# The last block of a weight load in six partition pieces: the tail of a gated attention and FFN kernel on Trainium2

## The chip, the cores and the metric

The kernel runs on one core of a Trainium2 chip. The metric is the device time of one execution in microseconds (us). It is taken from several runs, and their median counts. One further execution is recorded by the hardware profiler, and all rows below come from that one.

## What is computed

The reference mixes two branches over a batch of two tokens (D = 448) with a sigmoid gate: attention over a cache of 4096 positions with 16 heads of 256, and a feed-forward layer with 1792 hidden units. Everything is in float32.

```python
x = A_x
g = _sigmoid((x * gate_w).sum(-1, keepdims=True))
# a: q = x @ wq; scores = q . k_cache * 256 ** -0.5; softmax; o = p . v_cache; a = o @ wo
a = _A_ref(x, A_k_cache, A_v_cache, A_wq, A_wo)
# b: h = x @ w1 + b1; h = relu(h) ** 2; b = h @ w2 + b2
b = _B_ref(x, B_w1, B_b1, B_w2, B_b2)
return g * a + (1 - g) * b
```

The K and V caches are 268 MB of the 290 MB that are read, so nearly all of the run is one long stream of loads.

## The kernel before

The work is cut into 16 rounds; a round is two heads of one batch entry. Each round loads a K tile and a V tile of 128 partitions x 16384 floats. VectorE multiplies K by q in place (`times_q`, L282) and sums the rows (`row_sums`, L288); a maximum over partitions and an exponential give the softmax; TensorE multiplies the probabilities with V (`values`, L333). Three large tiles (`kp0`, `kp1` for K in turn, `vp` for V) fill the memory on the chip, so that each load waits until the tile that it overwrites has been used.

All large loads are issued by hand, in program order, on the queue of SP (SyncE). Each load is tied to one of eight landing semaphores (`DMAHW0` to `DMAHW7`), in turn, and these are shared by all loads and stores. A load is issued only when the load that had the same semaphore before it, eight places earlier, has landed.

The end of the program is what matters here. When the last K tile has been used, the remaining weights go into its place, `kp1`: `load_wo` (L115) brings the last part of wo, then `load_v` (L132) the last V tile into `vp` in five loads cut at `V_CUTS = (32, 48, 56, 60)` of 64 rows, and `load_w2` (L98) all of w2. w2 is laid out as 128 partitions x 14 blocks x 448 floats (`"(p c) n -> p c n"`): partition p holds 14 consecutive rows of w2, and block c is one of them from each partition, 1792 bytes per partition. `W2_CUTS = (2, 6, 10, 13)` makes five loads of it: blocks 0-1, 2-5, 6-9, 10-12 and the single block 13 (224 KB).

TensorE's order at the end is written by hand too: the five pieces of the last `values`, then `late_w2(0, 2)`, the turn of the last attention output (`take_turn`), `late_wo` for two heads, and `late_w2(2, FC)` for blocks 2 to 13. `late` (L379) multiplies a 128x2 operand with four slices of 112 columns of a block and adds into the accumulator `fin`. Each block is four such matrix products, which the trace shows as eight weight loads and eight matmuls. ScalarE copies `fin` out (L498), and SP and ScalarE store one batch row each (L500, L501).

Of the kernel before, what the change touches and what calls it, by code (L numbers as in the profile page):

```python
# [16 lines left out]
def kernel(  # L17
# [14 lines left out]
    nc = tc.nc  # L32
# [13 lines left out]
    FC = F // P  # L46
# [6 lines left out]
    W2_CUTS = (2, 6, 10, 13)  # L53
# [33 lines left out]
    w2_v = w2.rearrange("(p c) n -> p c n", c=FC)  # L87
    w2_sb = {}

    def load_w2():  # L90

        at = HJ * D
        tv = kp[last % 2][:, at:at + FC * D].rearrange("p (c n) -> p c n", n=D)
        for c in range(FC):
            w2_sb[c] = tv[:, c, :]
        cuts = [0, *W2_CUTS, FC]
        for lo, hi in zip(cuts, cuts[1:]):
            nc.sync.dma_start(tv[:, lo:hi, :], w2_v[:, lo:hi, :])  # L98

# [375 lines left out]
    load_wo(NG - 1, last)  # L477
    vt_next = load_v(i + 1, vp, V_CUTS)
    load_w2()
    values(i, vt, 0, NK // 4)  # L480
    mt = maximum(i + 1)
# [8 lines left out]
    cuts = [0, *(c // 2 for c in V_CUTS), NK // 2]  # L490
# [38 lines left out]
```

## Time and profile before

| what | value |
|---|---|
| median of 3 runs | 680.91 us (680.66 to 680.99) |
| the profiled execution's own time | 680.71 us |
| its span on the core | 678.9 us |
| read from memory | 289.56 MB, 427 GB/s over the span |
| VectorE busy | 573.2 us (84%) |
| TensorE matmul busy | 245.9 us (36%) |
| ScalarE busy | 35.5 us (5%) |

The span runs from the first to the last event on the core; the execution's own time is 1.8 us longer. The chain of waits is read back from the last instruction, at each step to whatever released it. The DMA share is the mean over the 16 engines that move data: 0.25 means that about four of the sixteen are at work. PE is TensorE's matmul, PEld its weight loads, DVE VectorE, ACT ScalarE, SP SyncE, and a q behind a name (SPq) is that engine's instruction queue. PE's busy times are modelled and overlap.

### The profile page before, as it was taken

What the parts mean: (1) busy time and instruction counts of PE and PEld (TensorE: products, weight loads), DVE (VectorE), ACT (ScalarE), POOL (GpSimd) and SP (SyncE); (2) the same over time, 40 slices, a digit from 0 to 9 for tenths busy, and PEclk for the clock granted to TensorE, in tenths of its full rate; (3) what the DMA queues carried; (4) which work ended last, traced back from release to release, by engine and by line L of the source; (5) the groups of instructions that cost most, each with busy time, mean ns of one, the idle gap of its engine ahead of it and who ended that gap; (6) DMA issues with size and microseconds to landing.
All of it is one profiled execution on the core that took longest, in us unless ns stands there. A gap on an engine that the chain in (4) does not pass through costs nothing.

```text
span 678.9 us, 3814 instructions
## 1 busy us (share of the span) xinstructions
PE 245.9 (36%) x1658; PEld 78.9 (12%) x1658; DVE 573.2 (84%) x150; ACT 35.5 (5%) x116; POOL 0.7 (0%) x6
## 2 busy tenths in 40 slices
PE   2522250503308541240515644050512550602476
PEld 1100210100104110010101301010100310100122
DVE  3069999999899995979989895998989799999920
ACT  0001000000001000000000100000000200100000
POOL 0000000000000000000000000000000000000000
PEclk9956575665757656575856578575655775755789
DMA  9999999999999999999999999999999999999996
GB/s 379 440 421 441 440 430 444 432 440 437 429 436 407 452 432 432 432 433 432 432 430 432 436 432 433 432 437 432 432 432 432 412 458 413 426 456 432 399 423 267
DMA packets 7628, 289.80 MB, mean 427 GB/s; under 512 B 950, under 2 KB 1084, under 8 KB 2364
## 3 DMA queue, kind: packets, MB, share of 16 engines
q1 hardware_dynamic: 7448, 289.54, 98.9%
q8 instruction: 13, 0.21, 0.1%
q10 hardware_dynamic: 164, 0.02, 0.0%
q14 instruction: 3, 0.02, 0.0%
HBM read 289.56 MB, written 0.00 MB: 427 GB/s over the span
## 4 chain that ended last, share of the span: by engine, by line
DVE 47%; DMA 44%; issue 6%; PE 3%; ACT 0%; SPq 0%; DVEq 0%; ACTq 0%
DMA kp<-in_A_k_cache_dram 32%; DVE kp L282 25%; DVE s L288 21%; DMA vp<-in_A_v_cache_dram 9%; DMA kp<-in_B_w_dram 2%; PE po_buf L333 2%; PE mt L296 0%; DVE pw L434 0%; PE fin L379 0%; ACT pw L307 0%; DVE m L292 0%; PE sum L313 0%; DVE nb L302 0%; SPq L77 0%; DVE hb L270 0%
## 5 line engine op out<-in xcount | busy, mean ns | idle before, releaser
L282 DVE TENSOR_TENSOR kp<-kp,q 128x8192 f32<-128x8192 f32 (+2 forms) x34 | 278.2, 8182 | 53.2 <-DMA kp<-in_A_k_cache_dram 53.2
L288 DVE TENSOR_REDUCE s<-kp 128x32 f32<-128x8192 f32 x32 | 277.9, 8686 | 1.1
L333 PE MATMUL po_buf<-vp,pw 128*16 128x512 f32 (+1 forms) x960 | 140.9, 747 | 219.1 <-DMA vp<-in_A_v_cache_dram 219.1
L333 PEld LDWEIGHTS po_buf<-vp,pw 128*16 128x16 f32 (+1 forms) x960 | 31.0, 112 | 324.2 <-issue 248.3
L296 PE MATMUL mt<-ident,m 128*64 128x64 f32 x64 | 7.3, 317 | 138.9 <-DVE m L292 138.9
L374 PE MATMUL acc<-kp,oT 128*2 128x448 f32 x48 | 26.8, 730 | 18.8 <-issue 18.8
L307 ACT ACTIVATE pw<-s,nb 64x64 f32<-64x64 f32 x32 | 11.1, 347 | 388.6 <-DVE nb L302 388.4
L296 PEld LDWEIGHTS mt<-ident,m 128*64 128x64 f32 x64 | 4.8, 192 | 149.6 <-issue 127.6
L355 PE MATMUL ot<-rl,shared 128*128 128x8 f32 x96 | 17.0, 307 | 3.8 <-ACT shared L350 3.4
L355 PEld LDWEIGHTS ot<-rl,shared 128*128 128x128 f32 x96 | 16.1, 253 | 7.2 <-ACT shared L350 7.2
L238 PE MATMUL pq<-qs,ident 128*64 128x256 f32 x64 | 14.1, 529 | 0.7 <-ACT qs L226 0.7
L200 PE MATMUL ph<-vp,xT 128*4 128x448 f32 x28 | 7.2, 679 | 17.3 <-DMA vp<-in_B_w_dram 17.3
L333 PE MATMUL po_buf<-kp,pw 128*8 128x512 f32 x64 | 9.6, 752 | 8.7 <-DMA kp<-in_A_v_cache_dram 8.7
L302 DVE TENSOR_REDUCE nb<-mt 128x1 f32<-128x64 f32 x16 | 3.6, 224 | 10.7 <-PE mt L296 10.7
L350 ACT ACTIVATE shared<-po_buf 128x512 f32<-128x512 f32 x12 | 6.5, 594 | 86.5 <-PE po_buf L333 81.1
L200 PE MATMUL po_buf<-vp,xT 128*4 128x512 f32 x56 | 7.8, 714 | 4.9 <-DMA vp<-in_A_wq_dram 4.9
L241 ACT ACTIVATE q<-pq 128x256 f32<-128x256 f32 x16 | 6.1, 383 | 62.5 <-PE pq L238 62.3
L374 PEld LDWEIGHTS acc<-kp,oT 128*2 128x2 f32 x48 | 4.8, 103 | 38.9 <-issue 38.9
L319 DVE RECIPROCAL rc<-sum 128x8 f32<-128x8 f32 (+1 forms) x5 | 1.0, 196 | 9.2 <-PE sum L313 9.2
L307 ACT ACTIVATION_READ_ACCUMULATOR pw<-s,nb 64x1 f32 x32 | 5.9, 184 | 0.0
L434 DVE MEMSET pw<- 128x512 f32 x10 | 4.8, 485 | 0.6
L238 PEld LDWEIGHTS pq<-qs,ident 128*64 128x64 f32 x64 | 4.4, 176 | 4.2 <-issue 2.3
(61 smaller groups left out, 58.1 us busy)
## 6 DMA issues: line engine op xcount, KB each, us to landing
kp<-in_A_k_cache_dram SPq DMA_DIRECT2D x4, 4096.0 KB, 27.6
vp<-in_A_wq_dram SPq DMA_DIRECT2D x1, 7168.0 KB, 19.5
kp<-in_A_wo_dram SPq DMA_DIRECT2D x4, 1792.0 KB, 25.5
vp<-in_A_v_cache_dram SPq DMA_DIRECT2D x1, 4096.0 KB
vp<-in_B_w_dram SPq DMA_DIRECT2D x1, 3136.0 KB
vp<-in_A_v_cache_dram SPq DMA_DIRECT2D x1, 2048.0 KB, 30.7
kp<-in_B_w_dram SPq DMA_DIRECT2D x2, 896.0 KB, 27.4
vp<-in_A_v_cache_dram SPq DMA_DIRECT2D x1, 1024.0 KB
```

Of the source, the lines that this page charges most:

```text
L200: nc.tensor.matmul(out[32 * g:32 * g + 2 * B, :width], xT[:, half, c].rearrange("p s b -> p (s b)"), t[:, (a * n + g) * width:(a * n + g + ...
L238: nc.tensor.matmul(pq[k * PH:(k + 1) * PH, :DH], ident[:, r:r + 1].to_broadcast([P, PH]), qs[:, k * DH:(k + 1) * DH], start=True, stop=True)
L241: nc.scalar.activation(q_sb[i], pq[:, :DH], AF.Copy)
L282: nc.vector.tensor_tensor(kt, kt, q_sb[i].unsqueeze(1).to_broadcast([P, hi - lo, DH]), op=ALU.mult)
L288: nc.vector.tensor_reduce(s_t[i][:, at], rows(kp[i % 2])[:, at, :], axis=AX.X, op=ALU.add)
L296: nc.tensor.matmul(mt[at, :PH], m.to_broadcast([P, PH]), ident[:, at], start=True, stop=True)
L307: nc.scalar.activation(pw[b][at, :, 2 * c:2 * c + 2], s_t[i][at].rearrange("p (m s) -> p m s", s=2), AF.Exp, bias=nb[at], accum_out=rs_t[u ...
L333: nc.tensor.matmul(po[r:r + 4 * n, :], pw[b][:, m, :4 * n], vt[:, 2 * m:2 * m + 2, :].rearrange("p j d -> p (j d)"), start=(k == 0 and b = ...
L350: nc.scalar.activation(o_w[:, s], pv[:, s, lo:lo + nj // 2].unsqueeze(2).to_broadcast([P, nj // 2, HG, HP]), AF.Copy)
L355: nc.tensor.matmul(ptv[:, lo + j, :], ov[:, s, j, :], rl_t[u][:, :, s], start=(s == 0), stop=(s == 1))
L374: nc.tensor.matmul(acc[:, :D], oT[g][:, j, :], wo_sb[g][:, j, :], start=False, stop=(g == NG - 2 and j == HJ - 1))
L434: nc.vector.memset(pw[b], 0.0)
```

## The change

The first four loads of w2 stay. Block 13, which was one load over all 128 partitions, becomes six loads of 64, 36, 14, 8, 4 and 2 partitions, one behind the other on the same queue. Their bytes add up to the same 224 KB and go to the same places.

```diff
-        cuts = [0, *W2_CUTS, FC]
+        cuts = [0, *W2_CUTS]
         for lo, hi in zip(cuts, cuts[1:]):
             nc.sync.dma_start(tv[:, lo:hi, :], w2_v[:, lo:hi, :])
+
+        p = 0
+        for n in (64, 36, 14, 8, 4, 2):
+            nc.sync.dma_start(tv[p:p + n, hi:, :], w2_v[p:p + n, hi:, :])
+            p += n
```

The end of SP's queue before: the load of wo, the five of V, the five of w2, the store. `kp_69` and `kp_70` are the two K tiles, and a name such as `DMAHW4_49` is a landing semaphore that is waited for.

```order
L115 DMA kp_70<-in_A_wo_dram 128x4x896 [waits DMAHW6_49,DVE_49]
L132 DMA vp<-in_A_v_cache_dram 128x8192 [waits DMAHW0_49,PE_49]
L132 DMA vp<-in_A_v_cache_dram 128x4096 [waits PE_49]
L132 DMA vp<-in_A_v_cache_dram 128x2048 [waits DMAHW5_49,PE_49]
L132 DMA vp<-in_A_v_cache_dram 128x1024 [waits PE_49]
L132 DMA vp<-in_A_v_cache_dram 128x1024 [waits DMAHW7_49,PE_49]
L98 DMA kp_70<-in_B_w_dram 128x896
L98 DMA kp_70<-in_B_w_dram 128x1792 [waits DMAHW1_49]
L98 DMA kp_70<-in_B_w_dram 128x1792 [waits DMAHW2_49]
L98 DMA kp_70<-in_B_w_dram 128x1344 [waits DMAHW3_49,DVE_49]
L98 DMA kp_70<-in_B_w_dram 128x448 [waits DMAHW4_49]
L500 DMA out_dram<-shared 4x112 [waits DMAHW6_49,Activation_49]
```

The same place with the change, from the fourth load of w2 on:

```order
L98 DMA kp_70<-in_B_w_dram 128x1344 [waits DMAHW3_49,DVE_49]
L102 DMA kp_70<-in_B_w_dram 64x448 [waits DMAHW4_49]
L102 DMA kp_70<-in_B_w_dram 36x448 [waits DMAHW5_49]
L102 DMA kp_70<-in_B_w_dram 14x448 [waits DMAHW6_49]
L102 DMA kp_70<-in_B_w_dram 8x448 [waits DMAHW7_49]
L102 DMA kp_70<-in_B_w_dram 4x448 [waits DMAHW0_49]
L102 DMA kp_70<-in_B_w_dram 2x448 [waits DMAHW1_49]
L505 DMA out_dram<-shared 4x112 [waits DMAHW3_49,Activation_49]
```

Six issues stand where one stood, and each waits for a landing of its own. The one of 64 partitions waits, as the whole block did, for the second load of the last V tile; those of 36, 14 and 8 wait for the third, fourth and fifth V load, that of 4 for w2's blocks 0-1, that of 2 for w2's blocks 2-5. The store's wait moves from the fourth V load to w2's blocks 10-12.

TensorE's last products (`late_w2`, L379 before and L384 after) before:

```order
L379 MATMUL fin<-kp_70,hT 2x112 [waits DMAHW2_49]
L379 MATMUL fin<-kp_70,hT 2x112 x15
L379 MATMUL fin<-kp_70,hT 2x112 [waits DMAHW3_49]
L379 MATMUL fin<-kp_70,hT 2x112 x11
L379 MATMUL fin<-kp_70,hT 2x112 [waits DMAHW4_49]
L379 MATMUL fin<-kp_70,hT 2x112 x3
L524 UNCONDITIONAL_BRANCH
```

With the change:

```order
L384 MATMUL fin<-kp_70,hT 2x112 [waits DMAHW2_49]
L384 MATMUL fin<-kp_70,hT 2x112 x15
L384 MATMUL fin<-kp_70,hT 2x112 [waits DMAHW3_49]
L384 MATMUL fin<-kp_70,hT 2x112 x11
L384 MATMUL fin<-kp_70,hT 2x112 [waits DMAHW5_49,DMAHW6_49,DMAHW4_49,DMAHW7_49,DMAHW1_49,DMAHW0_49]
L384 MATMUL fin<-kp_70,hT 2x112 x3
L529 UNCONDITIONAL_BRANCH
```

The products and their order are the same. The first product of block 13 waits for six landings instead of one; one wait rides on the instruction, and the other five are carried by three separate wait instructions ahead of it on TensorE's queue.

## Rows read from the trace of the kernel before

**Rows 1.** The page: the span in 40 slices, the DMA lines.

```profile
DMA  9999999999999999999999999999999999999996
GB/s 379 440 421 441 440 430 444 432 440 437 429 436 407 452 432 432 432 433 432 432 430 432 436 432 433 432 437 432 432 432 432 412 458 413 426 456 432 399 423 267
DMA packets 7628, 289.80 MB, mean 427 GB/s; under 512 B 950, under 2 KB 1084, under 8 KB 2364
```

**Rows 2.** The chain of waits, its last steps: start us, us, what.

```profile
587.62 36.40 DMA vp<-in_A_v_cache_dram
...
630.87 26.74 DMA vp<-in_A_v_cache_dram
...
657.67 16.94 DMA kp<-in_B_w_dram
674.60 0.04 issue
674.65 0.99 PE fin L379 x32
...
675.72 0.26 ACT shared L498
```

**Rows 3.** Timeline of TensorE's last stretch: start, length, engine, line, count, idle before.

```profile
665.02 1.05 PE L333 MATMUL po_buf<-vp,pw 128*8 128x512 f32 x8 [0.34 <-DMA vp<-in_A_v_cache_dram]
666.30 1.03 PE L333 MATMUL po_buf<-vp,pw 128*8 128x512 f32 x4 [0.23 <-DMA vp<-in_A_v_cache_dram]
667.58 1.03 PE L333 MATMUL po_buf<-vp,pw 128*8 128x512 f32 x4 [0.25 <-DMA vp<-in_A_v_cache_dram]
668.65 0.30 PEld L379 LDWEIGHTS fin<-kp,hT 128*2 128x2 f32 x16 [0.97 <-DMA kp<-in_B_w_dram]
673.02 0.95 PE L379 MATMUL fin<-kp,hT 128*2 128x112 f32 x32 [0.56 <-DMA kp<-in_B_w_dram]
674.65 0.95 PE L379 MATMUL fin<-kp,hT 128*2 128x112 f32 x32 [0.68 <-DMA kp<-in_B_w_dram]
```

**Rows 4.** Landing of block 13's load, issued at 662.5 (window 662.5 to 662.6).

```profile
L98 SPq DMA_DIRECT2D kp<-in_B_w_dram x1: 328/328/328, 662.5 to 662.5; - x1
DMA to landing us min/median/max: 12.6/12.6/12.6
```

**Rows 5.** Timeline of the weight loads, from 675.15 to 675.30.

```profile
675.20 0.13 PEld L379 LDWEIGHTS fin<-kp,hT 128*2 128x2 f32 x8
```

**Rows 6.** Stretches at the end: us, busy by engine, granted clock, DMA share, GB/s.

```profile
662.00:670.00 8.00, 6.98 (x66) 1.73 (x58) 0.00 (x0) 0.60 (x1) 0.00 (x0) 1.00 1.02 413
670.00:671.50 1.50, 1.23 (x37) 1.15 (x40) 0.00 (x0) 0.18 (x1) 0.00 (x0) 1.00 1.00 406
671.50:673.50 2.00, 1.44 (x62) 1.18 (x57) 0.00 (x0) 0.00 (x0) 0.00 (x0) 1.00 0.59 237
673.50:674.20 0.70, 0.47 (x20) 0.20 (x9) 0.00 (x0) 0.00 (x0) 0.00 (x0) 1.00 0.22 90
674.80:675.20 0.40, 0.40 (x24) 0.34 (x17) 0.00 (x0) 0.00 (x0) 0.00 (x0) 1.00 0.00 0
```

**Rows 7.** DMA packets of two stretches, 673.5 to 674.2 and 662 to 670.

```profile
DMA packets 23, 0.06 MB, mean 90 GB/s; under 512 B 4, under 2 KB 15, under 8 KB 23
...
DMA packets 699, 3.30 MB, mean 413 GB/s; under 512 B 77, under 2 KB 77, under 8 KB 661
```

**Rows 8.** What SP's queue waited for at L98, in the whole run.

```profile
SPq L98 <- DMA vp<-in_A_v_cache_dram: 13.9, 2, 9.4
```

**Rows 9.** Landing of w2's blocks 2-5, issued at 643.4 (window 643.3 to 643.5).

```profile
L98 SPq DMA_DIRECT2D kp<-in_B_w_dram x1: 328/328/328, 643.4 to 643.4; - x1
DMA to landing us min/median/max: 27.4/27.4/27.4
```

**Rows 10.** The stores at the end: timeline, then SP's last waits.

```profile
676.01 0.65 SPq L500 DMA_DIRECT2D out_dram<-shared  x1
...
SPq L524 <- DMA out_dram<-shared: 1.1, 1, 1.1
```

**Rows 11.** The line L379: count, ns min/median/max, first and last start.

```profile
L379 PE MATMUL fin<-kp,hT x112: 257/259/259, 668.7 to 675.3; 128*2 128x112 f32 x112
...
L379 PEldq EVENT_SEMAPHORE  x1: 51/51/51, 650.4 to 650.4; - x1
```

## The prediction

> **What bounds the kernel now.** I read the page's DMA lines first [rows 1]: the DMA engines are busy in 39 of 40 slices at 427 GB/s, so the kernel is a stream of loads, and only the last slice is thinner. Then the end of the chain of waits [rows 2]: from 587.62 to 674.60 us it is nearly all DMA. Its last DMA step is the important one. It begins with an issue at 657.67 and lands at 674.60. That load is blocks 10-12 of w2, the one ahead of block 13. The chain goes through it to 32 matmuls (0.99 us), which are blocks 10 to 13, eight matmuls each, and to the copy at 675.72. The load that the change cuts up is not in the chain.
>
> How far is it from the chain? Block 13 is issued at 662.5 and takes 12.6 us [rows 4]: it lands at about 675.1. TensorE starts blocks 10-12 at 674.65 and runs all 32 matmuls in one unbroken group of 0.95 us [rows 3]. One matmul is shown with 0.26 us [rows 11], and they overlap, so the 32 starts spread over 0.95 - 0.26 = 0.69 us. The 25th, the first of block 13, starts 24/31 of that later, 0.53 us, at 675.18; block 13's weight loads begin at 675.20 [rows 5]. Landing and readiness thus fall within 0.1 us of each other, and the trace shows no idle time of TensorE between them. So **earlier is worth at most 0.1 us, later costs nearly in full**.
>
> Why does block 13 land half a microsecond after the three blocks ahead of it, and not at once? The stretches show it [rows 6]: until 671.5 all 16 DMA engines work (share 1.00), then the share falls to 0.59, and between 673.5 and 674.2 to 0.22, 3.5 engines of 16. In that stretch just four packets under 512 B pass [rows 7], the closing records of four engines. So about four engines run more than a microsecond late, and they carry the last rows of blocks 10-12 and then eight rows each of block 13. After 674.8 nothing moves [rows 6].
>
> **The change part by part.** *The bytes* are the same, and the load of blocks 10-12 stays ahead in the same queue with the same wait. It lands at 674.60 as before: 0.
>
> *What it could gain.* If the six pieces give the late engines fewer rows, block 13 lands earlier. A row of 1792 bytes takes one engine 1792 / (427 GB/s / 16) = 0.067 us [rows 1]. Even with no row of block 13 on the late engines, the gain at the landing is 8 x 0.067 = 0.54 us, and TensorE, busy with blocks 10-12 until 675.18, can use 0.1 us of it at most. Gain on the path: 0 to 0.1, I take 0, since the 32 matmuls run without a break. This is the main point of the forecast.
>
> *The issues.* SP issues six loads of 0.33 us [rows 4] instead of one: 5 x 0.33 = 1.6 us more on SP, with nothing queued behind them but the store, which waits for the copy at 675.72 anyway. Each of the six waits for an earlier landing. The first passes at 662.5, where the whole block was issued [rows 4], after the second of two waits for V's loads, 13.9 us together [rows 8]. Those of 36, 14 and 8 partitions pass when TensorE can start on V's third to fifth load, at 665.0, 666.3 and 667.6 [rows 3]; that of 4 when blocks 0-1 are there, at 668.6 [rows 3]; that of 2 when blocks 2-5 land, at 643.4 + 27.4 = 670.8 [rows 9]. From issue to landing, the nearest row for a small transfer is the output: issued at 676.01, and over before the span ends at 678.9, so under 2.9 us with the program's end in it [rows 10]. The last two rows are thus there by 670.8 + 2.9 = 673.7, 1.4 us before the whole block landed. Cover: the late engines' backlog to 674.2. Cost 0.
>
> *The closing records.* Each engine now closes up to six loads instead of one. In the eight microseconds from 662 to 670, 77 such small records pass among 699 packets and the share stays at 1.02 [rows 6, 7], so they leave no hole. I bound them from above by a row's own time: 5 x 0.067 = 0.34 us on one engine; from below 0. I take 0, nearer to that stretch.
>
> The Trainium skill speaks against the change here ("DMA: Bandwidth & Descriptors", section "Rules for kernel authors"): under 64 KB a transfer is mostly overhead, and two transfers to disjoint halves of the partitions should be one over 128. With the fixed 2.0 us that the same page of the Trainium skill fits to a transfer on another issue path (section "Anatomy of one DMA"), five more in a row would be, as an estimate, +10 us and the sum 691 us.
>
> *The waits on TensorE.* Three separate wait instructions now stand between block 12 and block 13. One such took 51 ns [rows 11], so 0.15 us. They start once block 12's weight loads are out, before 675.2, and overlap matmuls that still run: 0 to 0.15 us on the path, I take 0.05.
>
> *Where the rows go* the trace does not show: no narrow load of this size is in it. Evenly spread, no engine gets more than 8 rows or so, and the cost is 0. Unevenly, a late engine pays 0.067 us for each row over 8. The other twelve have closed blocks 10-12 by 673.5 and have (675.1 - 673.5) / 0.067 = 24 rows to spare. Ends: 0, and the four small pieces (28 rows) on one late engine on top of an even 6 rows of the two large ones, 34 - 8 = 26 rows, 1.75 us. I take 0: [rows 6] show the loads over 128 partitions on all 16 engines, and the piece of 64 is half the block.
>
> **The sum** against the profiled execution: 680.71 + 0.05 = 680.76 us. That execution lies 0.20 us under the median of the runs (680.91); for the median the forecast is 680.96, rounded **681.0 us**. A measurement of this kernel tells about 0.2%, 1.4 us, from no change.
>
> **The rivals.**
> 1. *The late engines get more rows than now.* Narrow pieces may sit on few engines, and these may be the late ones. With half as many rows again, 12 instead of 8, and the closing records bounded as above: 4 x 0.067 + 0.34 = 0.6 us, 681.6. For: about four engines are late, and no row tells which. Against: they are four of sixteen, and the closing records left no hole. Still within 0.2%. Chance 0.10. The Trainium skill ("DMA: Bandwidth & Descriptors", section "Why a DMA increments its semaphore by 16 and not by 1") says that a load runs on the largest number up to 16 that divides its partitions, on the lowest-numbered engines. By that rule the pieces use 16, 12, 14, 8, 4 and 2 engines, and an engine gets from 11 rows (the first two) to 4 (the last two). As an estimate that is this rival with 0.2 us in rows if the late ones are first, and the forecast if they are last.
> 2. *A pile on one late engine*: slower. The 28 rows of the small pieces go through one late engine: +1.75, 682.7. It decides from 8 rows on a late engine, or about 32 on another. For: the pieces of 2 and 4 cannot fill 16 engines in whole rows. Against: it needs pieces of 14 and 8 on one engine too. Chance 0.03.
> 3. *The loads close one after the other*: slower. If a load moved only once the one ahead of it had closed, each of five more would add what a small transfer takes from issue to landing, at most 2.9 us [rows 10]: +14.5, 695. It decides from any hole at a closing that the other engines cannot fill. Against: the share of 1.02 across 77 closings [rows 6, 7]. Chance 0.02. The Trainium skill's estimate of +10 us above is this rival at another price.
> 4. *The split does not move rows between engines*, that is each partition stays with the engine that served it. The landing stays at 675.1 and the time too: 681.0, one with the forecast in the sum.
> 5. *Faster.* It would need blocks 10-12 to land earlier as well, by 1.4 us for a gain that a measurement can tell: 679.5. Nothing in the change touches them. Chance 0.03, for a cause that the trace hides.
>
> **How the numbers follow.** Forecast with rival 4: 0.82; rival 1: 0.10; rivals 2 and 3: 0.05; rival 5: 0.03. Within 0.2%: 0.82 + 0.10 = 0.92; slower 0.05; faster 0.03. The range takes the spread of the runs around the forecast (the lowest, 680.66, less once more the 0.33 between lowest and highest, for another set of runs: 680.3) and reaches to rival 1 with its bound, 681.6.
>
> **What would show it.** In the new profile the chain should still end with the load of blocks 10-12, landing near 674.6, then 32 matmuls of 0.95 to 1.1 us. SP should issue the six pieces at about 662.5, 665.0, 666.3, 667.5, 668.6 and 670.8. TensorE's queue should show three waits of some 0.05 us. If the late engines got fewer rows, the DMA share near 674 falls and the last landing comes earlier, while the end stays. The prediction is wrong if TensorE waits for the last block, or if the landing of blocks 10-12 itself moves by more than a microsecond.

## The result and the profile after

The change made the kernel slower by 1.2 us: 682.06 us median (681.56 to 682.51, 19 runs) against 680.88 us (680.62 to 681.27, 19 runs). The ratio is 1.0017, with a 95% interval of 1.0010 to 1.0024. That is still under the 0.2% that the prediction called the limit of a measurement, but the interval does not take in 1, and the median lies above the forecast range (680.3 to 681.6). The profiled execution took 681.92 us with a span of 680.0 us, 1.1 us longer than the span before.

The chain of waits of the changed kernel, its last steps (start us, us, what):

```profile
634.25 33.27 DMA vp<-in_A_v_cache_dram
667.51 0.02 issue
667.53 8.57 DMA kp<-in_B_w_dram
676.10 0.14 issue
676.23 0.42 PE fin L384 x8
...
676.73 0.26 ACT shared L503
```

Each row here comes from one profiled execution of a kernel. Before, the chain ended with blocks 10-12 [rows 2]. Now it ends with a piece of block 13, the one issued at 667.5: the fourth, of 8 partitions. It lands at 676.10, 1 us after the whole block did before [rows 4]. TensorE's timeline shows that this is only the smaller part of the loss:

```profile
673.68 0.95 PE L384 MATMUL fin<-kp,hT 128*2 128x112 f32 x32 [1.25 <-DMA kp<-in_B_w_dram]
675.33 0.76 PE L384 MATMUL fin<-kp,hT 128*2 128x112 f32 x24 [0.69 <-DMA kp<-in_B_w_dram]
676.23 0.37 PE L384 MATMUL fin<-kp,hT 128*2 128x112 f32 x8 [0.15 <-DMA kp<-in_B_w_dram]
```

The same rows before stand at 673.02 and 674.65, the second with all 32 matmuls [rows 3]. So blocks 6-9 came 0.66 us later and blocks 10-12 0.68 us later, although both loads stand ahead of the pieces in the queue and were issued at the same times as before. Then the 32 matmuls fall apart: 24, a wait, 8. The copy moved from 675.72 [rows 2] to 676.73, by 1.01 us: **0.68 us before block 13 is touched, and 0.33 us for block 13 itself**.

SP issued the six pieces between 662.5 and 671.0 (all pieces of L102: count, ns, first and last start):

```profile
L102 SPq DMA_DIRECT2D kp<-in_B_w_dram x6: 232/295/581, 662.5 to 671.0; - x6
```

What happened to the loads ahead is seen in the stretches. Columns: us, busy by engine, granted clock, DMA share, GB/s. Before, between 671.5 and 672.5:

```profile
671.50:672.50 1.00, 0.96 (x41) 0.69 (x32) 0.00 (x0) 0.00 (x0) 0.00 (x0) 1.00 0.71 287
```

With the change:

```profile
671.50:672.50 1.00, 0.93 (x40) 0.67 (x28) 0.00 (x0) 0.00 (x0) 0.00 (x0) 1.00 0.75 224
```

The packets of this stretch, before and with the change:

```profile
DMA packets 82, 0.29 MB, mean 287 GB/s; under 512 B 11, under 2 KB 43, under 8 KB 82
DMA packets 70, 0.22 MB, mean 224 GB/s; under 512 B 16, under 2 KB 40, under 8 KB 70
```

The DMA engines are as busy (share 0.75 against 0.71) and move a fifth less (224 against 287 GB/s). Each packet takes longer: 0.71 x 16 us of engine time over 82 packets is 0.14 us each, 0.75 x 16 us over 70 is 0.17 us, with packets that are no larger (3.2 KB against 3.5 KB on average). Nothing in the prediction had a place for that.

### The profile page after: what moved, and what is told of

Read it like the earlier page. It is cut to its first block, busy times and chain, and to the rows that moved or that the text cites. A ratio compares the mean times of both kernels' runs of the same rounds, so it can differ in the third digit from the quotient of the medians.

```text
span 680.0 us, 3822 instructions
## 1 busy us (share of the span) xinstructions
PE 241.2 (35%) x1658; PEld 76.3 (11%) x1658; DVE 573.2 (84%) x150; ACT 35.5 (5%) x116; POOL 0.7 (0%) x6
## 4 chain that ended last, share of the span: by engine, by line
DVE 47%; DMA 44%; issue 6%; PE 3%; ACT 0%; SPq 0%; DVEq 0%; ACTq 0%
DMA kp<-in_A_k_cache_dram 32%; DVE kp L287 25%; DVE s L293 20%; DMA vp<-in_A_v_cache_dram 10%; PE po_buf L338 3%; DMA kp<-in_B_w_dram 1%; PE mt L301 0%; DVE pw L439 0%; ACT pw L312 0%; DVE m L297 0%; PE sum L318 0%; PE fin L384 0%; SPq L77 0%; DVE nb L307 0%; DVE hb L275 0%
## 5 line engine op out<-in xcount | busy, mean ns | idle before, releaser
L338 PE MATMUL po_buf<-vp,pw 128*16 128x512 f32 (+1 forms) x960 | 138.9, 736 | 220.7 <-DMA vp<-in_A_v_cache_dram 220.7
L379 PE MATMUL acc<-kp,oT 128*2 128x448 f32 x48 | 24.6, 678 | 18.4 <-issue 18.4
L360 PE MATMUL ot<-rl,shared 128*128 128x8 f32 x96 | 15.4, 289 | 4.0 <-ACT shared L355 3.5
L360 PEld LDWEIGHTS ot<-rl,shared 128*128 128x128 f32 x96 | 14.4, 230 | 7.5 <-ACT shared L355 7.5
L379 PEld LDWEIGHTS acc<-kp,oT 128*2 128x2 f32 x48 | 4.5, 98 | 36.5 <-issue 36.5
```

The source lines that it names most:

```text
L338: nc.tensor.matmul(po[r:r + 4 * n, :], pw[b][:, m, :4 * n], vt[:, 2 * m:2 * m + 2, :].rearrange("p j d -> p (j d)"), start=(k == 0 and b = ...
L360: nc.tensor.matmul(ptv[:, lo + j, :], ov[:, s, j, :], rl_t[u][:, :, s], start=(s == 0), stop=(s == 1))
L379: nc.tensor.matmul(acc[:, :D], oT[g][:, j, :], wo_sb[g][:, j, :], start=False, stop=(g == NG - 2 and j == HJ - 1))
```

## The experiments

Three theories were set against each other. *Crowding*: a load of 64 neighbouring partitions is moved by all 16 DMA engines but writes only into the part of the memory on the chip that 8 of them served before; packets get longer, those of the loads ahead too. *Rows*: only the number of rows and closings on the late engines matters. *Count*: each further load costs, whatever it covers. The times of the kernel before that were taken on the same chip are 680.98 us for the first four runs and 681.06 us for the last two. The times of one kernel spread over 0.6 to 1.4 us and each interval is about 1.2 us wide, so the landings in the traces carry more of the argument than the times.

### Two halves of neighbouring partitions

```diff
-        p = 0
-        for n in (64, 36, 14, 8, 4, 2):
-            nc.sync.dma_start(tv[p:p + n, hi:, :], w2_v[p:p + n, hi:, :])
-            p += n
+        for s in (slice(0, 64), slice(64, 128)):
+            nc.sync.dma_start(tv[s, hi:, :], w2_v[s, hi:, :])
```

> Block 13 in two loads of 64 neighbouring partitions (0-63, 64-127). The change costs 1.2 us (682.06 against 680.88). Crowding theory: a load of 64 neighbouring partitions is moved by all 16 engines, but writes only into the half of the memory that 8 of them served before; packets of the loads ahead get longer too, and blocks 10-12 land later. Then two such loads cost about as much as the change: +0.5 to +1.3 us, and the moved bytes per busy engine fall under 300 GB/s somewhere between 671 and 674. Rows theory (late engines carry more rows and closings): each engine has 8 rows as before and one closing more: 0 to +0.1 us. Count theory (each further load costs): one load more, +0.2 us.

Measured: 681.71 us, ratio 1.0011 (1.0002 to 1.0019), +0.73 us. The load of blocks 10-12 in the chain, the end of TensorE's timeline and the same stretch:

```profile
657.62 17.69 DMA kp<-in_B_w_dram
...
675.36 1.06 PE L382 MATMUL fin<-kp,hT 128*2 128x112 f32 x32 [0.92 <-DMA kp<-in_B_w_dram]
...
671.50:672.50 1.00, 0.89 (x40) 0.62 (x28) 0.00 (x0) 0.00 (x0) 0.00 (x0) 1.00 0.77 220
```

Blocks 10-12 are as late as with the change (675.36 against 675.33), with two loads, none of them small, and with 8 rows of block 13 on each engine if the loads spread evenly. This is what crowding expected; rows and count expected at most 0.1 and 0.2 us. Its other sign came too: rate divided by share is 220 / 0.77 = 286 GB/s, under the 300 that it named.

### Two halves of every second partition

```diff
-        for s in (slice(0, 64), slice(64, 128)):
+        for s in (slice(0, 128, 2), slice(1, 128, 2)):
             nc.sync.dma_start(tv[s, hi:, :], w2_v[s, hi:, :])
```

> The same two loads of 64 partitions, but of every second partition (even ones, then odd ones), so that each load touches all parts of the memory evenly. Crowding theory: blocks 10-12 land as before the change, 0 to +0.3 us in all, clearly less than the two neighbouring halves. Rows theory: 0 to +0.1 us, the same as the neighbouring halves. Count theory: +0.2 us, the same as the neighbouring halves.

Measured: 680.95 us, ratio 1.0001 (0.9992 to 1.0010), no difference from the kernel before.

```profile
657.57 17.11 DMA kp<-in_B_w_dram
...
674.72 1.03 PE L382 MATMUL fin<-kp,hT 128*2 128x112 f32 x32 [0.69 <-DMA kp<-in_B_w_dram]
...
671.50:672.50 1.00, 0.86 (x37) 0.59 (x27) 0.00 (x0) 0.00 (x0) 0.00 (x0) 1.00 0.71 285
```

The two kernels differ in nothing but which 64 partitions go together: the same number of loads, bytes, waits and rows. Yet one has blocks 10-12 at 674.72, the other at 675.36, and the times are 0.76 us apart: ten of the eleven mixed runs are faster than the fastest run with neighbouring halves. That separates crowding from the two others.

### The six loads, spread over every second partition

```diff
-        p = 0
-        for n in (64, 36, 14, 8, 4, 2):
-            nc.sync.dma_start(tv[p:p + n, hi:, :], w2_v[p:p + n, hi:, :])
-            p += n
+        nc.sync.dma_start(tv[0:128:2, hi:, :], w2_v[0:128:2, hi:, :])
+        p = 1
+        for n in (36, 14, 8, 4, 2):
+            s = slice(p, min(p + 2 * n, 128), 2)
+            nc.sync.dma_start(tv[s, hi:, :], w2_v[s, hi:, :])
+            p += 2 * n
```

> Six loads of 64, 36, 14, 8, 4 and 2 partitions as in the change, with the same waits, engines and closings, but the first takes the even partitions and the others walk through the odd ones. Crowding theory: the landing of blocks 10-12 goes back to 674.6 to 675.0 (675.29 with the change), total +0.3 to +0.7 us against before, about half of the change's cost. Rows theory and count theory: the same +1.2 us as the change, since rows per engine, loads and waits are the same.

Measured: 681.68 us, ratio 1.0010 (1.0001 to 1.0019), +0.70 us, as crowding expected (0.3 to 0.7), at the upper end. The interval reaches 1.3 us and so takes in the 1.2 of the other two; the landing has to decide.

```profile
657.80 17.23 DMA kp<-in_B_w_dram
675.02 0.04 issue
675.07 0.76 PE fin L386 x24
675.82 0.10 issue
675.93 0.42 PE fin L386 x8
...
671.50:672.50 1.00, 1.00 (x48) 0.84 (x36) 0.00 (x0) 0.00 (x0) 0.00 (x0) 1.00 0.83 280
```

These are steps of its chain and the same stretch. Blocks 10-12 land at 675.02, just past the 674.6 to 675.0 that crowding expected. Their load was issued 0.13 us later than before in this execution (657.80 against 657.67 [rows 2]), so that from issue to landing 17.23 us stand against 16.94 before and 17.64 with the change (675.33 less 0.04 at the wait, less its issue at 657.65): more than half of the loss comes back. The rest fits loads that are still crowded, since the 36 odd partitions from 1 to 71 lie nearly all in the lower half and the other 28 in the upper; that was not tried apart. The gap between the 24 and the last 8 matmuls is here too.

### Ten loads over all 128 partitions

```diff
-    W2_CUTS = (2, 6, 10, 13)
+    W2_CUTS = (2, 5, 7, 8, 9, 10, 11, 12, 13)
```

This one starts from the kernel before.

> w2 in ten loads over all 128 partitions (cut after blocks 2, 5, 7, 8, 9, 10, 11, 12 and 13), as many loads as with the change and with waits like its own, the last issued when the second has landed. Crowding theory: no partition is moved to another engine, so the packets keep their length: -0.3 to +0.3 us. Count theory: five loads more, with late issues: +0.8 to +1.3 us, like the change. Rows theory: 8 rows per engine and block, five closings more on each engine: +0.3 us.

Measured: 681.40 us, ratio 1.0007 (0.9998 to 1.0016), +0.42 us. Just above what crowding expected (at most 0.3), nearest to the 0.3 of rows, and half of the least that count expected (0.8); the interval takes in no change, so that this run alone decides little. Its chain ends with the tenth load, which could be issued only at 670.34, when the second had landed:

```profile
670.34 5.08 DMA kp<-in_B_w_dram
675.43 0.04 issue
675.47 0.42 PE fin L379 x8
```

It lands 0.3 us after the last block of the kernel before (675.1 [rows 4]). Five further loads that cover all partitions thus cost 0.4 us here, at most 0.16% or 1.1 us by the interval, against the 1.2 us of the change.

### Three pieces

```diff
-        for n in (64, 36, 14, 8, 4, 2):
+        for n in (64, 36, 28):
```

> The change with its three loads of 64, 36 and 28 partitions: the four small pieces in one, issued at 666.3, so that no load waits for a landing of w2 itself. Crowding theory: the two wide neighbouring pieces do the harm, blocks 10-12 land at 675.2 to 675.4 as with the change (675.29); block 13 follows with one or two closings less: +0.7 to +1.1 us. Count theory (late issues and small loads): about half of the change's cost goes, +0.3 to +0.6 us.

Measured: 681.72 us, ratio 1.0013 (1.0004 to 1.0022), +0.66 us between the medians; the ratio, which is not that of the medians, makes it 0.9 us.

```profile
657.53 17.89 DMA kp<-in_B_w_dram
...
675.47 1.06 PE L384 MATMUL fin<-kp,hT 128*2 128x112 f32 x32 [0.80 <-DMA kp<-in_B_w_dram]
676.66 0.26 ACT L503 ACTIVATE shared<-fin 128x112 f32<-128x112 f32 x1 [6.09 <-PE fin L384]
...
671.50:672.50 1.00, 0.84 (x36) 0.58 (x25) 0.00 (x0) 0.00 (x0) 0.00 (x0) 1.00 0.86 242
```

Blocks 10-12 are as late as ever, without any load that waits for w2 itself. They land at 675.43, just past what crowding expected (675.2 to 675.4). The time lies between the two theories by the medians (crowding 0.7 to 1.1, count 0.3 to 0.6) and within crowding's range by the ratio, so the landing decides. The small pieces and their late issues are not what delays the loads ahead. What they add is open: the medians of this kernel and the change are 0.5 us apart against their own kernels before, the copies in the two traces only 0.07 us (676.66 and 676.73).

Side by side, the runs that cut only block 13 keep one order. The rate of the stretch divided by its share is 404 GB/s before, 401 with the mixed halves, 337 with the six spread loads, 299 with the change, 286 with the neighbouring halves and 281 with three pieces. From issue to landing, blocks 10-12 took 16.94, 17.11, 17.23, 17.64, 17.69 and 17.89 us. The lower the rate at which busy engines move, the later the load ahead.

### The crowding by itself

The V tile of round 5 in two loads of 64 neighbouring partitions, that of round 8 in two loads of every second partition, in the kernel before:

```diff
         at = [0, *cuts, NK]
+        split = {5: (slice(0, 64), slice(64, 128)), 8: (slice(0, 128, 2), slice(1, 128, 2))}
         for lo, hi in zip(at, at[1:]):
-            nc.sync.dma_start(rows(t)[:, lo:hi, :], of_round(v_cache, i)[:, lo:hi, :])
+            for s in split.get(i, (slice(0, 128),)):
+                nc.sync.dma_start(rows(t)[s, lo:hi, :], of_round(v_cache, i)[s, lo:hi, :])
```

> The crowding by itself, far from the tail and with enough bytes to see it: in the kernel before, the V tile of round 5 (8 MB, some 19.6 us at full rate) comes in two loads of 64 neighbouring partitions, that of round 8 in two loads of every second partition. Crowding theory: while round 5's halves move, the rate falls to about half, near 215 GB/s, so that V takes up to 39 us there and the run is 15 to 20 us longer; round 8 stays at 400 GB/s or more and costs under 2 us. Count theory and rows theory: neither round changes, both stay near 430 GB/s, +0 to +1 us.

Measured, one run: 703.87 us, +22.8 us. The page's rate over the span, in 40 slices of 17.6 us, shows it at a glance:

```profile
DMA  9999999999999999999999999999999999999996
GB/s 406 431 423 422 467 419 426 426 459 419 430 433 435 433 429 213 209 315 429 433 441 430 409 458 430 429 433 442 426 429 437 423 440 418 432 450 429 400 429 268
```

Two and a half slices at half the rate, and nowhere else. The stretches of the same run, with the neighbouring halves (issued at 255) and the mixed ones (issued at 395):

```profile
262.00:294.00 32.00, 0.00 (x0) 0.00 (x0) 25.66 (x3) 0.00 (x0) 0.00 (x0) 0.50 1.04 217
300.00:304.00 4.00, 0.00 (x0) 0.00 (x0) 3.04 (x1) 0.00 (x0) 0.00 (x0) 0.50 0.91 197
304.00:308.00 4.00, 0.00 (x0) 0.00 (x0) 0.00 (x0) 0.00 (x0) 0.00 (x0) 0.50 0.69 229
...
409.00:429.00 20.00, 8.53 (x20) 1.67 (x20) 19.97 (x3) 0.38 (x1) 0.00 (x0) 0.67 1.01 436
```

At 217 GB/s, 8.4 MB take 38.7 us instead of 19.5 at 430: +19.2, and most of the 22.8. The slow stretch lasts until the V tile has landed, at about 308. Taking 217 GB/s from 262 to 300, some 9.9 MB move in 46 us, so that part of the K load behind must be among them; at 430 they would take 23 us, and the difference of 23 is about the whole loss. The share stays at 1.04 through most of it. All engines are busy, at half the rate. The mixed halves land at about 429 (33.6 us after their issue), and the 8.4 MB before that come at 436 GB/s.

## Why the prediction was wrong

**The step that failed** is the first term of the sum: the load of blocks 10-12 "stays ahead in the same queue with the same wait. It lands at 674.60 as before: 0". The issue was the same, and the landing was not: TensorE started on it at 675.33, 0.68 us later. A load that stands behind in the queue slowed those ahead. The two meet because the 16 engines do not run in step: in the microsecond from 671.5 of the kernel before, 32 rows of block 13 (43 - 11 packets of 512 B to 2 KB) moved beside 39 larger ones of the blocks ahead. Which partitions go together decides whether that costs anything; the two halves that differ in nothing else show it, and round 5 at 217 GB/s.

Why 64 neighbouring partitions run at half the rate, no run here shows. The Trainium skill ("SBUF — State Buffer", section "Door 1: The DMA port swizzle (why `[64,N]` ≈ `[32,N]`)") states that partitions 0 to 63 cover 8 of the 16 ports. The trace agrees, with 217 GB/s against some 430. The choice of partitions also decides what is read, since 64 neighbouring ones of V are one head, 4 MB in one piece, and no run changes the one without the other. Against a limit on the reading side stand the loads of wo in the same run, 1.8 MB in one piece over all 128 partitions: apart from the three slices of round 5 and the last one, no slice is under 400 GB/s. Half the rate for 64 partitions would have been the missing rival of the forecast, with a time of its own.

Of the prediction's two signs of being wrong, one came: TensorE waited for the last block. The other, more than a microsecond at the landing of blocks 10-12, did not.

**"Where the rows go"** asked only how many rows an engine gets, and bounded it by a pile on one engine. It did not ask where they are written. Even the counting came out against the change. The page after has 40 more packets under 512 B, the closing records (its DMA line; before 950 [rows 1]):

```profile
DMA packets 7668, 289.80 MB, mean 426 GB/s; under 512 B 990, under 2 KB 1124, under 8 KB 2404
```

Six loads have 16 + 40 = 56 closings between them. That fits the Trainium skill's rule ("DMA: Bandwidth & Descriptors", section "Why a DMA increments its semaphore by 16 and not by 1"), by which they run on 16, 12, 14, 8, 4 and 2 engines: the sum is 56. And the last packets of the run tell which engines are late. From 673.8 to 675 before, and from 674.5 to 676.2 with the change:

```profile
DMA packets 44, 0.09 MB, mean 75 GB/s; under 512 B 8, under 2 KB 40, under 8 KB 43
DMA packets 52, 0.08 MB, mean 48 GB/s; under 512 B 17, under 2 KB 50, under 8 KB 51
```

Before, 8 closings and 40 - 8 = 32 rows are four engines with two closings and 8 rows each. With the change there are 17 closings and 50 - 17 = 33 rows of block 13. By that rule, four late engines as before [rows 7] give 4 closings of blocks 10-12, then 4 for each of the pieces of 64, 36 and 14, and 1 for the piece of 8: 17. Rows: 4 x (4 + 3 + 1) + 1 = 33. So, by these counts, all four late engines are among the twelve that the piece of 36 uses, one of them among the eight of the piece of 8, and none among the four that get few rows. They carry 33 rows instead of 4 x 8 = 32, and each closes four or five loads instead of two. This is rival 1, with a quarter row more per engine instead of the four it priced; it was given 0.10.

**"The closing records" and "the waits on TensorE"**, 0 and 0.05 us in the forecast, belong to the other 0.33 us. TensorE would have been ready for block 13 at 675.33 + 0.53 = 675.86 by the prediction's own working; the piece of 8 landed at 676.10, 0.24 us later, and from there to the first matmul passed 0.14 us instead of 0.04 to 0.05 at a simple wait [rows 2]. The trace shows the three separate waits as foreseen, 51 ns each, with one earlier wait in the count:

```profile
L384 PEldq EVENT_SEMAPHORE  x4: 51/51/51, 649.7 to 676.1; - x4
```

How the 0.24 us split between the closings, the one row more and the rate was not tried by itself. The closings left no hole in the full stream [rows 6, 7]; that nothing else hides them on a late engine at the very end is argued and not shown. Crowding has a part in it too: in the neighbouring halves, with one closing more and no row more, block 13 landed at about 676.0, some 0.7 us after blocks 10-12 (675.31). That gap was 0.5 us before and with the mixed halves, and 0.8 us with the change (676.10 less 675.29).

**What held.** The six issues came where they were worked out, 662.5 to 671.0, and those of the two smallest pieces were not in the chain. No gain came, as forecast; that an earlier landing of block 13 is worth nothing was not tried, for no run landed it earlier (the mixed halves at about 675.2, and 680.95 us against 680.98). The loss of the sizes of rivals 2 and 3 did not come. The prediction's "later costs nearly in full" was right and then not followed through to the loads ahead.

**No version beat the kernel before.** The mixed halves equal it; the four others with w2 cut differently took 0.4 to 0.7 us more, and the change the most.

## What to carry to other kernels

When a load is split by partitions, ask not only how many engines move a piece but which partitions it writes: 64 neighbouring ones ran at half the rate here, every second one at the full rate. A load behind in a queue was not behind on every engine, so a slow one at the end also delayed the last pieces of those ahead. A term of zero for "the same load in the same place" needs a look at what follows it.

## What had not been expected

The DMA share does not tell a stream at full rate from one at half: 1.04 at 217 GB/s and 1.01 at 436 in the same run. Only the GB/s beside it does. And the end of the stream is uneven in the same manner in both kernels: four engines finish more than a microsecond after the other twelve, before [rows 6, 7] and after (with the change, no row of block 13 moves between 674.0 and 674.3, and the last one ends at about 675.4). Why it is these four was not tried.
